# The last 512 queries in two halves, and B's transposing loads held until A's first x has landed

## The chip, the cores and the metric

One core of one Trainium2 chip. The metric is device time in microseconds (us); a kernel is run several times, and the median is quoted with the lowest and highest run. TensorE is PE in the profile, ScalarE is ACT, VectorE is DVE, GpSimd is POOL, SyncE is SP; SPq is the queue on which SyncE issues transfers. L1031 is line 1031 of the kernel's file. The change shifts the lines, so the same statement has another number before and after it: the exponentials are L806 before and L820 after.

## The reference

Two independent attention modules on 2048 positions of 448 columns, set side by side in the output.

```python
def _A_ref(x, wq, wk, wv, wo):        # 16 query heads, one shared key/value head of 28
    q = (x @ wq).reshape(B, S, 16, 28).transpose(0, 2, 1, 3)
    k = x @ wk;  v = x @ wv
    scores = jnp.einsum("bhqd,bkd->bhqk", q, k) * (28 ** -0.5)
    p = _softmax(scores, axis=-1)
    o = jnp.einsum("bhqk,bkd->bhqd", p, v)
    return o.transpose(0, 2, 1, 3).reshape(B, S, 448) @ wo

def _B_ref(x, wqkv, wo):              # window of 8 keys, 2 apart; 16 heads of 28
    ...                               # q, k, v from x @ wqkv; gather; softmax; weighted sum; @ wo

return jnp.concatenate([a, b], axis=-1)
```

A has 16 x 2048 x 2048 exponentials; that is the kernel's main work. B is small and is worked between A's steps.

Some words of the kernel: the scores are the products of queries and keys, PV is the product of the exponentials with the values. A *unit* is one head's scores of 512 queries with 128 keys. A *quad* is four heads with the same 512 queries, 64 units. An *offload* is a tile of exponentials that VectorE works in place of ScalarE. Warm-up matmuls are dummies before the first real one.

## The kernel before

The kernel is a list of operations with their reads `R` and writes `W`; a scheduler with its own model of durations (the second argument of `a(...)`, in us) orders them on each engine and sets the semaphores.

`xst` is A's first 512 rows of x, loaded plainly and transposed by TensorE; the other rows of A's x (`xT_A`) and all of B's (`xT_B`) come by transposing loads of 128x512, four for each chunk of 512 rows, all on SyncE's queue.

```python
        a("act", 0.5, <A_x[0:512] -> xst>, W=["xst"], dsem="i_xa0", ...)
        ...
        a("gp", 1.5, wload(g.wq, g.A_wq, KC, D), ..., dsem="i_wq", ...)       # rest of A's query weights
        for c in range(1, NCH):
            for t in range(4):
                a("sp", 1.05, <transposing load>, R=["xst"], W=[("xT", c, t)], dsem=f"i_xa{c}.{t}", ...)
        for c in range(NCH):
            for t in range(4):
                a("sp", 1.05, <transposing load>, W=[("xT_B", c, t)], dsem=f"i_xb{c}.{t}", ...)
        ...
        a("gp", 1.5, <B's value weights>, W=["wqv"], dsem="i_wbv", land=5, pr=-7, ninc=2)
        ...
        a("sp", 0.6, <zero rows of Vst[0] -> v_dram>, R=[("Vst", 0)], W=[("vd", -1)], dsem="i_vz", land=2.5, pr=3, rel=4)
```

`R=["xst"]` on A's transposing loads is no read: they come from memory. It makes them wait until `xst` has landed, so that they don't take bandwidth from it. `Vst` is a buffer that B's values go through. B's values go through a two-deep buffer `Vst`, whose first slot also serves, zeroed, as the source of the zero rows; and B's products live in the same bytes as `xst`:

```python
        self.xst = self.stage[:, 0:4 * D].rearrange("p (b c) -> p b c", c=D)
        self.prodT = self.stage[:, :].rearrange("p (t w c) -> p t w c", t=4, w=WIN)
        ...
            op = a("dve", t_dve_2x(1024), <product q*k>, R=R, W=[("prodT", t)], pr=pr, rel=T)
            if k == 0:
                op.deps.update(g.s.rd.get("xst", ()))   # the first products overwrite xst
```

The tail of A, before: the last 512 queries of the last four heads are worked like any other quad, 64 units of exponentials and one PV bank (one of the buffers that TensorE's results go to); at the end the normalization is split into two halves of 256 columns, both after the last PV. `OFF_AT` says which exponentials VectorE takes over from ScalarE (66 tiles of 512 columns).

Of the kernel before, what the change touches and what calls it, by code (L numbers as in the profile page):

```python
# [6 lines left out]
ALU = mybir.AluOpType  # L7
# [22 lines left out]
XBANKS = (6, 7)  # L30
TAILB = (0, 1, 2, 4)
WARM = 7
QT = 27.0
# [5 lines left out]
OFF_AT = {q: (0, 2, 5, 7) for q in range(1, 16)}  # L39
OFF_AT.update({q: (0, 2, 3, 5, 7, 8) for q in (5, 9, 13)})  # L40
LATE = 2
# [52 lines left out]
class Sched:  # L94
# [49 lines left out]
    def run(self, engines):  # L144
# [44 lines left out]
        while left:  # L189
# [77 lines left out]
            if e == "pe":  # L267
                if o.use is not None and o.use.spare and o.alone and area(T) < (self.WANT if limit is None or T + o.dur + 0.18 <= limit + self.EPS else self.LOW):
                    o.fill = 1
                    o.dur += 0.18  # L270
                    o.dense += 512 - o.use.spare
                elif (o.full and area(T) < (self.FULL[o.full] if T + 0.22 * o.full + 0.2 <= H + self.EPS else self.LOW)
                      and all(d.start is not None and d.end + self.lat(d) <= T for d in o.opt)):
                    o.deps.update(o.opt)
                    o.dur = 0.22 * o.full
                    o.tiled = False
                    o.dense = 512 * o.full
                elif o.fill is not None:
                    o.full = 0
                    o.fill = max(0, min(0 if waiting else 2, round((self.WANT - area(T)) * self.WIN / 512 + 0.3)))  # L280
                    if T > 14 and area(T) > self.LOW:
                        o.fill = max(0, min(o.fill, int((H - 0.12 - self.MODE - T - o.dur + self.EPS) / 0.22)))
                    o.dur += 0.22 * o.fill
                    o.dense += 512 * o.fill
                if o.tiled and not mode:
                    o.dur += self.MODE
                mode = o.tiled
                if o.dense:
                    recent.append((T + o.dur, o.dense))
                    del recent[:-120]  # L290
# [108 lines left out]
class Gen:  # L399
# [185 lines left out]
    def loads(self):  # L585
# [20 lines left out]
        for c in range(NCH):  # L606
            for t in range(4):
                a("sp", 1.05, one(lambda e, c=c, t=t: e.dma_start(
                    out=g.xT_B[:, t, 512 * c:512 * c + 512], in_=g.B_x[0, 512 * c:512 * c + 512, XB0[t]:XB0[t] + 128],
                    transpose=True)), W=[("xT_B", c, t)], dsem=f"i_xb{c}.{t}", land=4.5, pr=-16 + c)  # L610
        a("sp", 1.2, lambda e: [
# [113 lines left out]
    def a_q(self, sc, first=False):  # L725
# [3 lines left out]
        for t in range(4):  # L729
# [16 lines left out]
            else:  # L746
# [11 lines left out]
              R=["qadd"], W=[("qT", par, t)], use=u, pr=pr if first else -1)  # L758

    def a_loop(self):  # L760
        g, a = self, self.s.add
        units = [(sc, t, tb, j) for sc in range(4) for t in range(4) for tb in range(16) for j in range(4)]
        assert len(units) == NU
        g.last_exp, g.pvs, g.evacs = {}, {}, []
        quads = {(sc, t): [[] for _ in range(4)] for sc in range(4) for t in range(4)}
        dqs = {k: [[] for _ in range(4)] for k in quads}
# [5 lines left out]
        while pos < NU:  # L772
# [9 lines left out]
            def qk(e, us=us, b0=b0, box=[]):  # L782
                for _ in range(box[0].fill):
                    e.matmul(g.bank(b0), g.warm[:, 0:128], g.warm[:, :], start=True, stop=True)
                for i, (sc, t, tb, j) in enumerate(us):
                    if box[0].full:
                        r = e.matmul(g.bank(b0 + i), g.kz[:, j, 128 * tb:128 * tb + 128], g.qT[:, sc % 2, t, :], start=True, stop=True)  # L787
                        continue
                    r = e.matmul(g.bank(b0 + i), g.kT[32 * j:32 * j + 32, 128 * tb:128 * tb + 128],  # L789
                                 g.qT[32 * j:32 * j + 32, sc % 2, t, :], start=True, stop=True, tile_position=(32 * j, 0))  # L790
                return r
            box = []
            o = a("pe", 0.315, lambda e, qk=qk, box=box: qk(e, box=box), R=[("kT", tb // 4) for (_, _, tb, _) in us] + [("qT", sc % 2, t) for (sc, t, _, _) in us],
                  W=[("ring", slot)], pr=-50)
            box.append(o)
            o.ring = o.tiled = True
            o.full = len(us) if len(us) > 1 else 0
            o.opt = {x for (_, _, tb, _) in us for x in g.kz_ops[tb // 4]}
            o.fill = 0
# [10 lines left out]
            for i in range(na):  # L810
                g.last_exp[b0 + i] = x
                quads[us[i][:2]][us[i][3]].append((us[i], ("expT", n % ERING), g.expT[:, n % ERING, 512 * i:512 * i + 512], 0))
            if off:
# [4 lines left out]
            while late and late[0][0] <= n // 2:  # L818
                for x in late.pop(0)[1]:
                    qd = x[0][:2]  # L820
                    g.nq[qd] = g.nq.get(qd, 0) + 1
# [9 lines left out]
            for u in us:  # L831
                js = quads[u[:2]]
                while all(js):
                    g.pv_group([x.pop(0) for x in js])
                if u[2:] == (15, 3):
                    left = [x.pop(0) for x in js if x]
# [3 lines left out]
    def pv_group(self, grp):  # L840
        g, a = self, self.s.add
        qd = grp[0][0][:2]
        all_pv = g.pvs.setdefault(qd, [])
        box = []

        def pv(e):
            for (_, _, tb, j), _, src, w in grp:
                order = [o.seq for o, js in all_pv if j in js]
                first, last = box[0].seq == min(order), box[0].seq == max(order)
                x = e.matmul(g.bank(PVBANK, p0=32 * j, p1=32 * j + 32), g.v_aug[:, w, tb, :], src,  # L850
                             start=first, stop=last, tile_position=(0, 32 * j))
            return x
        o = a("pe", 0.315, pv, R=sorted({y[1] for y in grp}) + sorted(
            {(k, y[3], y[0][2] // 4) for k in ("v_aug", "v_aug1") for y in grp}), pr=-40, dense=700)
        o.tiled = o.pv = True
# [5 lines left out]
        g.npv[qd] = g.npv.get(qd, 0) + len(grp)  # L861
        if g.npv[qd] == 64:
            g.a_quad_end(*qd)

    def offload(self, n, us):

        g = self
        if n % 2 or us[0][:2] != us[-1][:2]:
            return 0
        if us[0][:2] != g.quad:  # L870
            g.quad, g.round = us[0][:2], n // 2
        return int(n // 2 - g.round in OFF_AT.get(4 * us[0][0] + us[0][1], ()))

# [26 lines left out]

    def a_quad_end(self, sc, t):
        g, a = self, self.s.add
        end = 12.0 + QT * (4 * sc + t + 1)
        last = sc == 3 and t == 3
        evacs = []
        hv = 2 if last else 1
        for hf in range(hv):
            w, b = 512 // hv, 16 // hv
            cs, bs = slice(w * hf, w * hf + w), slice(b * hf, b * hf + b)
            keys = [hf] if last else [0, 1]  # L910
            kk = lambda n: [(n, t % 2, x) for x in keys]
            p0 = -30 if last else -1
            o = a("dve", t_dve_ps(w), lambda e, cs=cs: e.transpose(out=g.PV_T[:, t % 2, cs], in_=g.bank(PVBANK)[:, cs]),  # L913
                  W=kk("PV"), pr=-30)
            o.deps.update(x for x, _ in g.pvs[sc, t])
            evacs.append(o)
            pt = g.PV_T[:, t % 2, :].rearrange("p (b e) -> p b e", e=32)
            a("dve", 0.25, lambda e, pt=pt, bs=bs: e.reciprocal(out=g.rden[:, t % 2, bs], in_=pt[:, bs, DH]),
              R=kk("PV"), W=kk("rden"), pr=p0)
            a("dve", t_dve_1x(w), lambda e, pt=pt, bs=bs: e.tensor_tensor(  # L920
                out=g.oN[:, bs, :], in0=pt[:, bs, :], in1=g.rden[:, t % 2, bs].unsqueeze(2).to_broadcast([128, b, 32]), op=ALU.mult),
              R=kk("PV") + kk("rden"), W=[("oN", x) for x in keys], pr=p0)
            a("dve", 0.12 + 1.04e-3 * w, lambda e, cs=cs: e.transpose(
                out=g.oTn[:, t, cs], in_=g.oN[:, :, :].rearrange("p b e -> p (b e)")[:, cs]),
              R=[("oN", x) for x in keys], W=[("oTn", t, x) for x in keys], pr=p0)
        g.evacs = evacs
        pr = end + 20
        if t < 3:
            return
        for s4 in range(4):  # L930
            blk = 4 * sc + s4
            if last:
                u = Use(f"F{sc}.{s4}", (TAILB[s4],), late=True)
            else:
                u = Use(f"F{sc}.{s4}", XBANKS)
            for tt in range(4):
                o = a("pe", t_mm(D), lambda e, u=u, s4=s4, tt=tt: e.matmul(  # L937
                    g.bank(u.bank, D), g.oTn[:, tt, 128 * s4:128 * s4 + 128], g.wo4[:, tt, :], start=tt == 0, stop=tt == 3),
                  R=[("oTn", tt, s4 // 2), "wo4"], W=[u], use=u, pr=pr + s4 + tt if not last else -30 + tt, dense=448)
                if last and tt == 0:  # L940
                    o.deps.add(g.last_exp[TAILB[s4]])
            ob = blk % 4
# [195 lines left out]
```

## Time and profile before

| | before |
|---|---|
| device time, median of the runs | 461.0 us (460.56 to 461.34) |
| profiled span | 459.2 us |
| first exponential starts | 11.29 us |
| last exponential ends | 451.72 us |
| from there to the end | 7.5 us |
| granted TensorE clock | 1.00 |

The prediction below shows how ScalarE is read as the bound. Two more views are needed for what follows. First the timeline of SyncE's queue; the columns are start, length, engine, line, operation, tiles and count:

```profile
5.84 16.61 SPq L603 DMA_TRANSPOSE xT_A<-in_A_x_dram  x12
...
46.46 0.39 SPq L626 DMA_DIRECT2D v_scratch<-Vst  x1
```

Three of B's loads are issued ahead of these twelve (1.9 to 5.8 us), thirteen behind. Each takes 1.30 us of the queue, although the scheduler counts 1.05, and the store of the zero rows comes at 46.46 us.

Second, the DMA view, by queue: packets, MB and share of the 16 engines' time. q1 carries SyncE's transfers, q0 GpSimd's. First 4 to 8 us, then 12 to 14 us:

```profile
q1 hardware_dynamic: 2179, 0.51, 84.2%
```

### The profile page before, as it was taken

To read this page: it belongs to the slowest core of one execution; us is meant where nothing else is said; L and a number is where in the kernel's file an instruction comes from. 1 tells how busy PE (TensorE), PEld (TensorE's weight loads), DVE (VectorE), ACT (ScalarE), POOL (GpSimd) and SP (SyncE) were. 2 spreads that over 40 slices of the span, in tenths; PEclk is the share of its full clock that TensorE was granted. 3 is DMA by queue.
4 is the path that set the end of the run, shared out by engine and by line. 5 is a ranking of instruction groups with operands and counts; after the bars stand their busy time and mean duration, and the time that the engine had idled before them with its cause. 6 is when DMAs were issued, how large, how long until landed. Compare 5 with 4: busy or idle time off the path is not lost.

```text
span 459.2 us, 8717 instructions
## 1 busy us (share of the span) xinstructions
PE 427.7 (93%) x3682; PEld 163.6 (36%) x3682; DVE 380.7 (83%) x622; ACT 444.9 (97%) x430; POOL 9.4 (2%) x29
## 2 busy tenths in 40 slices
PE   8999999999999989999899999899899998989997
PEld 3333232323533324234353342224244342325343
DVE  6556889988798898989688889998988969889883
ACT  3999999999999999999999999999999999999994
POOL 7000000000000000000000000000000000000000
PEclk9999999999999999999999999999999999999999
DMA  7774303002201002020220120002022221214001
GB/s 152 128 162 95 109 27 100 1 1 90 92 15 40 19 10 82 20 81 22 81 91 30 44 83 18 0 13 92 0 97 92 70 78 30 72 31 142 10 1 61
DMA packets 42102, 27.34 MB, mean 60 GB/s; under 512 B 17474, under 2 KB 41904, under 8 KB 42064
## 3 DMA queue, kind: packets, MB, share of 16 engines
q1 hardware_dynamic: 40464, 25.28, 19.6%
q0 software_dynamic: 304, 0.73, 0.6%
q10 hardware_dynamic: 1296, 0.79, 0.5%
q8 instruction: 29, 0.48, 0.4%
q14 instruction: 9, 0.07, 0.1%
HBM read 17.60 MB, written 5.52 MB: 50 GB/s over the span
## 4 chain that ended last, share of the span: by engine, by line
ACT 86%; PE 11%; DVE 1%; DMA 1%; issue 0%
ACT expT L806 85%; PE ps L789 2%; PE ps L1079 2%; PE ps L850 2%; PE ps L787 1%; DMA stage<-in_A_x_dram 1%; PE ps L978 1%; PE ps L1086 1%; PE ps L937 1%; ACT e_t L1054 0%; PE ps L654 0%; PE ps L738 0%; PE ps L1028 0%; PE ps L434 0%; PE ps L993 0%
## 5 line engine op out<-in xcount | busy, mean ns | idle before, releaser
L806 ACT ACTIVATE expT<-ps 128x1024 bf16<-128x1024 f32 (+1 forms) x410 | 438.8, 1209 | 2.1 <-PE ps L789 1.9
L789 PE MATMUL ps<-qT,kT 32*128 32x512 bf16 x824 | 122.3, 385 | 11.6 <-ACT expT L806 9.3
L850 PE MATMUL ps<-expT,v_aug 128*32 128x512 bf16 x958 | 94.8, 389 | 1.0 <-ACT expT L806 1.0
L787 PE MATMUL ps<-qT,kz 128*128 128x512 bf16 x200 | 59.6, 383 | 9.9 <-ACT expT L806 9.4
L789 PEld LDWEIGHTS ps<-qT,kT 32*128 32x128 bf16 x824 | 30.1, 91 | 91.7 <-ACT expT L806 68.4
L883 DVE TENSOR_SCALAR d_x<-ps 128x512 f32<-128x512 f32 x66 | 45.4, 688 | 17.9 <-PE ps L789 16.8
L850 PEld LDWEIGHTS ps<-expT,v_aug 128*32 128x32 bf16 x958 | 24.3, 93 | 62.0 <-issue 55.4
L1073 DVE TENSOR_TENSOR prod<-Vsh,a_n 128x896 bf16<-128x896 bf16 x64 | 37.5, 614 | 7.9 <-PE ps L1079 7.9
L1019 DVE TENSOR_TENSOR stage<-qTB,kTB 112x1024 bf16<-112x1024 bf16 x64 | 42.3, 674 | 1.8 <-PE ps L1028 1.7
L1079 PE MATMUL ps<-ident,prod 128*112 128x128 bf16 x512 | 41.8, 224 | 0.0
L894 DVE SCALAR_TENSOR_TENSOR d_u<-d_u,d_x 128x1024 f32<-128x1024 f32 x33 | 40.1, 1215 | 0.1
L896 DVE SCALAR_TENSOR_TENSOR dexp<-d_u,d_x 128x1024 int16<-128x1024 f32 x33 | 40.0, 1213 | 0.1
L892 DVE SCALAR_TENSOR_TENSOR d_u<-d_x 128x1024 f32<-128x1024 uint16 x33 | 39.9, 1209 | 0.2
L1079 PEld LDWEIGHTS ps<-ident,prod 128*112 128x112 bf16 x512 | 34.2, 130 | 14.7 <-issue 10.9
L978 PE MATMUL ps<-xT_B,wqkv 128*128 128x512 bf16 x128 | 38.9, 383 | 0.0
L787 PEld LDWEIGHTS ps<-qT,kz 128*128 128x128 bf16 x200 | 12.2, 97 | 31.1 <-ACT expT L806 28.9
L1028 PEld LDWEIGHTS ps<-ones,stage 112*128 112x128 bf16 x512 | 18.5, 96 | 7.8 <-issue 4.8
L1028 PE MATMUL ps<-ones,stage 112*128 112x4 bf16 x512 | 21.2, 167 | 0.0
L738 PE MATMUL ps<-xT_A,wq 128*128 128x512 bf16 x64 | 19.8, 384 | 0.1
L1086 PE MATMUL ps<-wo_B,oT 112*128 112x448 bf16 x64 | 18.1, 357 | 0.0
L993 PE MATMUL ps<-wqv,xT_B 128*128 128x448 bf16 x64 | 17.5, 356 | 0.0
L913 DVE STREAM_TRANSPOSE PV_T<-ps 128x512 f32<-128x512 f32 (+1 forms) x17 | 11.4, 676 | 6.7 <-PE ps L850 6.5
(103 smaller groups left out, 303.3 us busy)
## 6 DMA issues: line engine op xcount, KB each, us to landing
Vsh<-v_scratch SPq DMA_DIRECT2D x16, 896.0 KB, 4.6
v_scratch<-Vst SPq DMA_DIRECT2D x16, 112.0 KB, 1.7
out_dram<-outB SPq DMA_DIRECT2D x16, 112.0 KB, 1.7
out_dram<-outA SPq DMA_DIRECT2D x14, 112.0 KB, 1.7
wqkv<-in_B_wqkv_dram SPq DMA_DIRECT2D x1, 672.0 KB, 5.4
stage<-in_A_x_dram ACTq DMA_DIRECT2D x1, 448.0 KB, 4.0
wo_B<-in_B_wo_dram SPq DMA_DIRECT2D x4, 98.0 KB
wo<-in_A_wo_dram SPq DMA_DIRECT2D x4, 98.0 KB
```

The lines of the kernel that those rows point to most:

```text
L787: r = e.matmul(g.bank(b0 + i), g.kz[:, j, 128 * tb:128 * tb + 128], g.qT[:, sc % 2, t, :], start=True, stop=True)
L789: r = e.matmul(g.bank(b0 + i), g.kT[32 * j:32 * j + 32, 128 * tb:128 * tb + 128], g.qT[32 * j:32 * j + 32, sc % 2, t, :], start=True, stop ...
L806: x = a("act", t_exp(w), lambda e, b0=b0, w=w, n=n: e.activation(g.expT[:, n % ERING, 0:w], g.ps[:, 512 * b0:512 * b0 + w], ACT.Exp, scale ...
L850: x = e.matmul(g.bank(PVBANK, p0=32 * j, p1=32 * j + 32), g.v_aug[:, w, tb, :], src, start=first, stop=last, tile_position=(0, 32 * j))
L883: o = a("dve", t_dve_ps(512), lambda e: e.tensor_scalar(out=xx[:, 512 * h:512 * h + 512], in0=g.bank(bank), scalar1=-128.0 * A2, scalar2=1 ...
L892: a("dve", t_dve_1x(1024), lambda e: e.scalar_tensor_tensor(out=u, in0=lo, scalar=EP * F, in1=lo, op0=ALU.add, op1=ALU.mult), R=di, W=["d_ ...
L894: a("dve", t_dve_1x(1024), lambda e: e.scalar_tensor_tensor(out=v, in0=u, scalar=EQ * F * F, in1=lo, op0=ALU.add, op1=ALU.mult), R=["d_u"] ...
L896: a("dve", t_dve_1x(1024), lambda e: e.scalar_tensor_tensor(out=out, in0=v, scalar=EL / F ** 3, in1=xx, op0=ALU.mult, op1=ALU.subtract), R ...
L978: a("pe", t_mm(512), lambda e, u=u, t=t, kt=kt, w=w: e.matmul(g.bank(u.bank), g.wqkv[:, kt, w * D + KC * t:w * D + KC * t + 128], g.xT_B[: ...
L1019: op = a("dve", t_dve_2x(1024), lambda e, t=t, qv=qv, kv=kv: e.tensor_tensor(out=g.prodT[0:KC, t, :, :], in0=qv, in1=kv, op=ALU.mult), R=R ...
L1028: r = e.matmul(g.bank(u.bank, 128).rearrange("p (h w) -> p h w", w=WIN)[:, 4 * t:4 * t + 4, w], g.prodT[0:KC, t, w, :], g.ones4[:, :], sta ...
L1079: a("pe", 0.056, lambda e, u=u, t=t, w=w: e.matmul(g.bank(u.bank, 128, 128 * t, p1=KC), g.prod2[:, w, KC * t:KC * t + KC], g.ident[:, :], ...
```

## The change

Its intent is to shorten both ends of the kernel. At the end, the last 512 queries of the last four heads become two halves of 256 queries, so that PV, normalization and output of the first half run beside the scores of the second, and only 256 columns are left after the last exponential. At the start, B's transposing loads get the same hold as A's. With it come fewer offloads (62), two more warm-up matmuls and a rule of the scheduler's model.

```diff
-TAILB = (0, 1, 2, 4)
-WARM = 7
+TAILB = (4, 0)
+WARM = 9
...
-OFF_AT.update({q: (0, 2, 3, 5, 7, 8) for q in (5, 9, 13)})
+OFF_AT.update({q: (0, 2, 3, 5, 7, 8) for q in (7,)})
+OFF_AT[15] = (0, 2, 3, 5)
...
-                if o.tiled and not mode:
+                if o.tiled and (not mode or o.fill):
                     o.dur += self.MODE
...
-                    transpose=True)), W=[("xT_B", c, t)], dsem=f"i_xb{c}.{t}", land=4.5, pr=-16 + c)
+                    transpose=True)), R=["xst"], W=[("xT_B", c, t)], dsem=f"i_xb{c}.{t}", land=4.5, pr=-16 + c)
...
+    def key(self, u):
+        return (3, 3, u[2] // 8) if u[:2] == (3, 3) else u[:2]
+    def parts(self, u):
+        if u[:2] == (3, 3):
+            return [(2 * (u[2] % 8) + i, 256 * (u[2] // 8), 256) for i in range(2)]
+        return [(u[2], 0, 512)]
... (scores, PV and the end of a quad go over parts(u) and key(u); the end of a quad takes hf = None, 0 or 1)
```

## The prediction

> **What bounds the kernel now.** I began with the page of the kernel before: busy time per engine, the row of ACT in the 40 slices, the chain that ended last, and the costliest group.
>
> ```profile
> PE 427.7 (93%) x3682; PEld 163.6 (36%) x3682; DVE 380.7 (83%) x622; ACT 444.9 (97%) x430; POOL 9.4 (2%) x29
> ...
> ACT  3999999999999999999999999999999999999994
> ...
> ACT 86%; PE 11%; DVE 1%; DMA 1%; issue 0%
> ...
> L806 ACT ACTIVATE expT<-ps 128x1024 bf16<-128x1024 f32 (+1 forms) x410 | 438.8, 1209 | 2.1 <-PE ps L789 1.9
> ```
>
> ScalarE (ACT) runs 410 exponentials and is idle 2.1 us around them, 1.9 of which come before the first. So the time has three parts: a **head** up to the first exponential, a **stream** of exponentials, and a **tail** after the last one. The timeline, cut to ACT, gives the borders, and the timeline of the last 8 us gives the tail:
>
> ```profile
> 11.29 5.97 ACT L806 ACTIVATE expT<-ps 128x1536 bf16<-128x1536 f32 x5 [1.90 <-PE ps L789]
> ...
> 434.81 16.91 ACT L806 ACTIVATE expT<-ps 128x1024 bf16<-128x1024 f32 x16
> ```
>
> ```profile
> 451.95 0.40 PE L850 MATMUL ps<-expT,v_aug 128*32 128x512 bf16 x4
> ...
> 452.41 0.78 DVE L913 STREAM_TRANSPOSE PV_T<-ps 128x256 f32<-128x256 f32 x2 [5.22 <-PE ps L850]
> 453.11 0.32 DVE L918 RECIPROCAL rden<-PV_T 128x8 f32<-128x8 f32 x2
> 453.34 0.72 DVE L920 TENSOR_TENSOR oN<-PV_T,rden 128x256 bf16<-128x256 f32 x2
> 453.99 0.76 DVE L923 STREAM_TRANSPOSE oTn<-oN 128x256 bf16<-128x256 bf16 x2
> 454.48 0.11 PEld L937 LDWEIGHTS ps<-wo,oTn 128*128 128x128 bf16 x2 [0.46 <-DVE oTn L923]
> ...
> 454.67 0.65 DVE L1082 CAST oT<-ps 112x512 bf16<-112x512 f32 x1
> ...
> 455.25 1.14 DVE L947 CAST outA<-ps 128x448 bf16<-128x448 f32 x2
> ...
> 456.35 0.62 DVE L1089 CAST outB<-ps 128x448 bf16<-128x448 f32 x1
> 457.00 0.33 SPq L1091 DMA_DIRECT2D out_dram<-outB  x1
> ```
>
> Head 11.29 us; stream 11.29 to 451.72 = 440.43 us; tail 451.72 to 459.2 = 7.5 us. In the tail VectorE (DVE) is the path: it works two 256-column halves of the last PV bank one beside the other, then the last evacuations of module B (oT, outB) queue with those of outA, and the outB store is the last thing issued.
>
> A second look at the stream matters, since a busy ACT can hide a wait. Within runs of exponentials the start-to-start times in the trace are 904 ns (1024 columns) and 1330 ns (1536) at their medians. 270 x 0.904 + 139 x 1.330 = 429.0 us; the stream ends another 0.7 us after the last start, so about 10.7 us of the 440.4 are not plain exponentials. Eight e_t exponentials (0.30 each) and four gcol ones explain about 3. The other 6 us sit in some 70 places of 0.03 to 0.25 us where the score matmuls ended later than 120 ns before the exponential could have begun. ACT waits for PE a little, and counts it as busy.
>
> **What the Trainium skill says.** "ScalarE: Activation LUTs", What ACT_TABLE_LOAD costs: an ACTIVATE streams one element per 0.833 ns, with a fixed part that back-to-back ones partly hide. The trace agrees: 1330 - 904 = 426 ns for 512 more columns, 0.832 each, so 50 ns per exponential is fixed. "TensorE: Matmul & The Clock Gate", Back-to-back issue gap: a warm matmul costs N/2.4 + 2.5 ns when it follows another, so halving one into two 256-column ones is nearly free (an estimate from that page: 218 against 216 ns); the trace has no 256-column matmul, but two full-array 512-column score matmuls start 215 to 225 ns apart. "TensorEngine Tiling (Array Packing)", Key Properties: tiles work independently; in the trace three 32-row score matmuls start within 7 ns and all end 0.39 us after the first start. "DMA: Bandwidth & Descriptors", Issuing engines are not separate DMA queues: all queues share the 16 engines; the trace agrees, below.
>
> **The change, part by part.**
>
> *Head.* Three transposing loads of B's x no longer run before A's first x has landed. The DMA view of the kernel before, cut to 3.4 to 3.9 us and then to 4.4 to 4.9 us (packets, MB, share of 16 engines; q10 carries the load of x, q1 the transposes):
>
> ```profile
> q10 hardware_dynamic: 225, 0.19, 108.7%
> q1 hardware_dynamic: 9, 0.00, 1.1%
> ```
>
> ```profile
> q1 hardware_dynamic: 256, 0.06, 64.2%
> q10 hardware_dynamic: 315, 0.07, 61.3%
> ```
>
> As the transposes arrive, q10 falls from 0.19 to 0.07 MB per half microsecond. Between 3.9 and 4.82 us it moved 0.16 + 0.07 MB; at 0.19 per half that is 0.6 us instead of 0.92, so x should land 0.3 us sooner. The 16 PE transposes, which wait for it 0.5 us, follow. The order of the built program also puts the four Q projections ahead of the second K projection, with two warm-up matmuls in the gap; worth about 0.1. A's later transposing loads start a microsecond sooner, which nothing waits for. Head: **-0.4 us**. B's loads come later, but their first use is at 38.0 us, and in the new order it still stands before the 25th exponential.
>
> *Stream.* Offloaded exponentials on DVE fall from 66 to 62: two fewer in each of quads 5, 9 and 13, two more in 7 (the last quad keeps four, all in its first half). Counted in the built program: 143 exponentials of 1536 and 266 of 1024 against 139 and 270. Four go from 904 to 1330 ns: 4 x 0.426 = **+1.7 us**. DVE loses 4 x 0.69 + 2 x (1.21 + 1.215 + 1.213) = 10 us, but beside ACT, so that is worth only what it takes off PE's waits.
>
> *Waits inside the stream.* In the last 32 units of two key blocks, a tiled score group is six 256-column matmuls, the two halves of one head one after the other in the same 32 rows. If they stagger in order I estimate 0.39 + 2 x 0.107 = 0.60 us. From the end of the exponential that frees the banks, a prompt group needs 0.055 + 0.60 + 0.046 = 0.70 us, and has 904 - 111 = 0.79 (the 111 is how far an exponential's record runs past the start of the next). It fits by 0.09, where a 512-column one has 0.30. But the median tiled group in the trace starts 0.23 us after the banks are free, because PE is finishing something else: such a one would now cost ACT about 0.1. Some 13 tiled groups, with PE freer than before (B's last work now stands before them): **+0.4 us**. Against it, less DVE work and a scheduler that counts a mode switch after each filler should take something off the 6 us: **-0.3 us**, the softest number here.
>
> *Tail.* Only 256 columns remain. From the end of the last exponential E: PV starts at +0.23 and DVE at +0.69 as before (eight 256-column PV matmuls in two rounds of four end when four of 512 do). Then one half alone: 0.41 + 0.16 + 0.39 + 0.43 with three 0.04 us gaps = 1.5, so oTn is ready at E+2.2 (before: E+2.7 and E+3.0). Last output matmuls +0.4; copies on ACT and DVE beside each other 0.6; the last store is issued at about E+3.4. Before it was 457.00 - 451.72 = E+5.3. From issue to the end stays 2.2 us. Tail: 5.6 instead of 7.5, **-1.9 us**. Module B's last 10 transposing matmuls, oT, projection and outB are gone from here: the order shows them before the second half.
>
> Sum: -0.4 + 1.7 + 0.4 - 0.3 - 1.9 = -0.5, from 461.0 to **460.5 us**.
>
> **The rivals.** (1) *The longer score groups stall ACT at every second exponential.* For it: 0.09 us of slack, and the schedule still takes them for 0.315 us long. Against it: with B gone PE idles before most groups, so they start promptly. Cost: up to 13 x 0.25 = 3 us, giving 463. (2) *The whole program is reordered, and the 6 us of small waits change.* Each is a near miss between two engines, so a new order draws new ones; the sign is open, the size perhaps 1 us each way, giving 459.5 to 461.5. (3) *The tail is hidden by another end*: if B's last store or the first half's outputs still came after E+3.4, the saving would vanish and the time be 462. The order speaks against it: B's last projection stands 21 score groups before the end. (4) *DVE sets the boundary between the halves*: the first half's last PV needs two DVE exponential chains (3.7 us each), and PE is in order, so a late chain blocks scores. I counted about 1 us to spare (chain done near 4.8 us after its scores, wanted at 5.7). Cost if late: about 1 us.
>
> **Range and chances.** The two large terms, +1.7 and -1.9, are counted and nearly cancel. The head is good to 0.3, the tail to 0.4, the small waits to about 1: 459.3 to 461.9 us eight times in ten. A 2% change is 9.2 us, as much as the whole tail and more; nothing in the change can give or take it. Within 2%: 0.98; 0.01 on each side.
>
> **What would show it.** First exponential at 10.9 us, and x landed near 4.5. 410 exponentials, the spacing sum up by 1.7. From the end of the last exponential to the end of the span 5.6 us, with outA as the last store and no L1098 or L1101 in the tail. Six-matmul score groups about 0.60 us long, and no idle time of ACT at the border of the halves. I am wrong if those groups cost ACT over 1 us in sum, if the small waits elsewhere move by more than 1.5 us, or if the head does not move.

## More of the kernel before

What an operation has to wait for comes from this rule:

```python
    def add(self, eng, dur, emit, R=(), W=(), pr=0.0, rel=0.0, ..., dsem=None, land=0.0, ...):
        for k in R:
            if k in self.wr:
                op.deps.add(self.wr[k])            # a reader waits for the last writer
            self.rd.setdefault(k, []).append(op)   # ... and is entered as a reader
        for k in W:
            ...
            op.deps.update(self.rd.get(k, ()))     # a writer waits for all readers
```

The loads that matter here.

```profile
q1 hardware_dynamic: 1181, 0.28, 73.6%
q0 software_dynamic: 83, 0.20, 31.6%
```

Between 4 and 8 us the transposes, most of them B's three, keep the DMA engines busy. This looks like interference with A's x, and is what the change wants to remove.

## The result, and the profile after

| | before | after |
|---|---|---|
| median of the runs | 461.0 us (460.56 to 461.34, 6 runs) | 465.57 us (464.8 to 469.8, 6 runs) |
| profiled span | 459.2 us | 462.8 us |
| first exponential starts | 11.29 us | 11.37 us |
| last exponential ends | 451.72 us | 457.08 us |
| from there to the end | 7.5 us | 5.8 us |
| granted TensorE clock, all runs | 1.00 | 0.976 to 0.999 |

The ratio is 1.0113, 95% interval 1.0076 to 1.015. Here and below a ratio is the mean time of one kernel's fast runs over that of the other's of the same rounds, so it is not quite the ratio of the medians. The changed kernel is slower by 1.1%, inside 2%, but outside the predicted range. Its times also spread over 5 us, where the kernel before spreads over 0.8.

The tail is as predicted. The timelines of ScalarE's last exponentials, and of VectorE behind them:

```profile
439.50 17.57 ACT L820 ACTIVATE expT<-ps 128x1024 bf16<-128x1024 f32 x16
```

```profile
457.58 0.45 DVE L926 STREAM_TRANSPOSE PV_T<-ps 128x256 f32<-128x256 f32 x1 [5.45 <-PE ps L866]
...
458.77 0.45 DVE L935 STREAM_TRANSPOSE oTn<-oN 128x256 bf16<-128x256 bf16 x1
...
459.67 0.62 DVE L959 CAST outA<-ps 128x448 bf16<-128x448 f32 x1 [0.46 <-PE ps L949]
```

One chain of 256 columns, then outA; nothing of module B is left there. The loss must lie in the stream (the exponentials between the first and the last). The costliest group of the page has grown an idle part (after the bar: idle time before the group, and what ended most of it):

```profile
L820 ACT ACTIVATE expT<-ps 128x1024 bf16<-128x1024 f32 (+1 forms) x410 | 440.2, 1231 | 6.0 <-PE ps L803 5.7
```

It was 2.1, of which 1.9 came before the first exponential. ScalarE's timeline from 44 us says where the rest is; the number in brackets is idle time just before:

```profile
50.10 2.52 ACT L820 ACTIVATE expT<-ps 128x1536 bf16<-128x1536 f32 x2 [2.68 <-PE ps L803]
53.94 6.46 ACT L820 ACTIVATE expT<-ps 128x1536 bf16<-128x1536 f32 x6 [1.31 <-PE ps L803]
```

Both waits name PE. PE's and VectorE's waits, and VectorE's timeline, lead further back:

```profile
PE ps L795 <- DVE d_x L899: 2.9, 1, 2.9
```

```profile
46.19 0.69 DVE L1031 TENSOR_TENSOR stage<-qTB,kTB 112x1024 bf16<-112x1024 bf16 x1 [2.89 <-DMA xT_B<-in_B_x_dram]
...
48.10 0.68 DVE L899 TENSOR_SCALAR d_x<-ps 128x512 f32<-128x512 f32 x1
```

Read upwards: ScalarE waits for scores, PE (which works in order) waits for VectorE to read a score bank at L899, and VectorE (in order too) sits 2.89 us in front of L1031, B's first product, until the *last* of B's transposing loads has landed. The product has no use for that load: its own operands were copied before. It waits because the hold entered B's sixteen loads as readers of `xst`, and the first product, which overwrites `xst`, waits for all readers. In the kernel before, VectorE came to the same product 7 us later, behind its first copy of B's values, and neither waited:

```profile
51.89 0.61 DVE L997 CAST Vst<-ps 128x448 bf16<-128x448 f32 x1
...
53.08 0.68 DVE L1019 TENSOR_TENSOR stage<-qTB,kTB 112x1024 bf16<-112x1024 bf16 x1
```

The second gap, 1.31 us, follows from the first. In the windows view (stretch; then busy us and count of PE, PEld, DVE, ACT, POOL; then PE's granted clock, DMA share, GB/s):

```profile
46.00:50.00 4.00, 1.10 (x10) 0.23 (x8) 3.81 (x7) 1.42 (x2) 0.00 (x0) 0.73 0.54 136
50.00:54.00 4.00, 4.00 (x20) 0.82 (x17) 2.24 (x3) 2.54 (x3) 0.00 (x0) 0.50 0.25 70
```

In the first stretch PE was busy 1.10 of 4 us and its clock fell to half; in the second it was busy all the time and still too slow. The trace's record of the granted clock has the fall at 47.85 us and full clock again at 54.68. "TensorE: Matmul & The Clock Gate", What's actually happening, has this state: half clock after an idle window of about 3.4 us, full clock after as long a busy one. The trace agrees with the half clock (0.50) and with the length: the 6.83 us at half clock are two times 3.41, and PE was busy 2.34 us of the first and all of the second.

SyncE's queue shows the same delay of everything behind the loads:

```profile
49.45 0.39 SPq L627 DMA_DIRECT2D v_scratch<-Vst  x1
```

That is 3.0 us later than before. This line plays a part only later.

To see losses in one number per stretch I took, from each trace, the start-to-start times of neighbouring exponentials and summed what goes beyond 904 ns (after one of 1024 columns) or 1330 ns (after one of 1536), by the stretch in which the later one starts. This "excess" is used for all experiments:

| excess, us | to 24 us | 24 to 45 | 45 to 60 | 60 to 80 | after 80 | sum |
|---|---|---|---|---|---|---|
| before | 0.1 | 0.6 | 0.3 | 0.3 | 9.4 | 10.7 |
| after | 0.1 | 0.9 | 4.4 | 0.5 | 8.5 | 14.5 |

After 80 us the changed kernel has even a little less. Nearly all that it lost is between 45 and 60 us.

### The profile page after: what moved, and what is told of

Read it like the earlier page. It is cut to its first block, busy times and chain, and to the rows that moved or that the text cites. A ratio compares the mean times of both kernels' runs of the same rounds, so it can differ in the third digit from the quotient of the medians.

```text
span 462.8 us, 8908 instructions
## 1 busy us (share of the span) xinstructions
PE 422.6 (91%) x3747; PEld 165.7 (36%) x3802; DVE 372.6 (81%) x613; ACT 445.8 (96%) x429; POOL 9.4 (2%) x29
## 4 chain that ended last, share of the span: by engine, by line
ACT 80%; PE 9%; SPq 8%; DMA 2%; DVE 1%; issue 0%; DVEq 0%
ACT expT L820 79%; SPq L609 4%; SPq L604 3%; PE ps L803 2%; PE ps L866 2%; PE ps L1091 1%; PE ps L800 1%; DMA stage<-in_A_x_dram 1%; PE ps L990 1%; DMA xT_B<-in_B_x_dram 1%; PE ps L1040 1%; ACT e_t L1066 1%; PE ps L1005 0%; PE ps L949 0%; PE ps L1098 0%
## 5 line engine op out<-in xcount | busy, mean ns | idle before, releaser
L803 PE MATMUL ps<-qT,kT 32*128 32x512 bf16 (+1 forms) x853 | 120.3, 375 | 13.0 <-ACT expT L820 10.8
L866 PE MATMUL ps<-expT,v_aug 128*32 128x512 bf16 (+1 forms) x1022 | 95.8, 378 | 0.7 <-DVE v_aug L718 0.5
L800 PE MATMUL ps<-qT,kz 128*128 128x512 bf16 (+1 forms) x204 | 57.6, 362 | 13.4 <-ACT expT L820 10.2
L899 DVE TENSOR_SCALAR d_x<-ps 128x512 f32<-128x512 f32 x62 | 42.7, 688 | 24.4 <-PE ps L803 23.5
L1031 DVE TENSOR_TENSOR stage<-qTB,kTB 112x1024 bf16<-112x1024 bf16 x64 | 42.6, 677 | 3.6 <-DMA xT_B<-in_B_x_dram 2.9
L1091 PE MATMUL ps<-ident,prod 128*112 128x128 bf16 x512 | 44.7, 225 | 0.0
L910 DVE SCALAR_TENSOR_TENSOR d_u<-d_u,d_x 128x1024 f32<-128x1024 f32 x31 | 37.7, 1215 | 0.2
L908 DVE SCALAR_TENSOR_TENSOR d_u<-d_x 128x1024 f32<-128x1024 uint16 x31 | 37.7, 1215 | 0.1
L912 DVE SCALAR_TENSOR_TENSOR dexp<-d_u,d_x 128x1024 int16<-128x1024 f32 x31 | 37.6, 1214 | 0.1
L990 PE MATMUL ps<-xT_B,wqkv 128*128 128x512 bf16 x118 | 36.8, 383 | 0.7 <-issue 0.6
L800 PEld LDWEIGHTS ps<-qT,kz 128*128 128x128 bf16 x235 | 15.3, 97 | 30.1 <-ACT expT L820 26.3
```

What stands on the lines that cost most here:

```text
L800: r = e.matmul(g.bank(b0 + i, nq, nq * k), g.kz[:, j, 128 * tb:128 * tb + 128], g.qT[:, sc % 2, t, q0:q0 + nq], start=True, stop=True)
L803: r = e.matmul(g.bank(b0 + i, nq, nq * k), g.kT[32 * j:32 * j + 32, 128 * tb:128 * tb + 128], g.qT[32 * j:32 * j + 32, sc % 2, t, q0:q0 + ...
L866: x = e.matmul(g.bank(PVBANK, nq, q0, p0=32 * j, p1=32 * j + 32), g.v_aug[:, w, tb, :], src[:, nq * k:nq * k + nq], start=first, stop=last ...
L899: o = a("dve", t_dve_ps(512), lambda e: e.tensor_scalar(out=xx[:, 512 * h:512 * h + 512], in0=g.bank(bank), scalar1=-128.0 * A2, scalar2=1 ...
L908: a("dve", t_dve_1x(1024), lambda e: e.scalar_tensor_tensor(out=u, in0=lo, scalar=EP * F, in1=lo, op0=ALU.add, op1=ALU.mult), R=di, W=["d_ ...
L910: a("dve", t_dve_1x(1024), lambda e: e.scalar_tensor_tensor(out=v, in0=u, scalar=EQ * F * F, in1=lo, op0=ALU.add, op1=ALU.mult), R=["d_u"] ...
```

## The experiments

All kernels gave correct results. Medians and ranges are of all runs; ratios leave out runs over 1.5% above the fastest of their kernel, which are the slowest run of e10 and that of e11. The kernel before was timed on the same chip in the same rounds; its median there was 460.69 to 460.9 us. In e1, e2, e3, e5, e10, e11 and e13 to e15 every engine but SyncE keeps the order of instructions of the kernel that is edited; the others are scheduled anew.

### Is it the first product's wait? (e1_narrow, e2_wait15)

The theory: the wait at L1031 is the whole loss. e1 lets the product wait only for TensorE's reads of `xst`, which are the real ones; e2 leaves out only the very last load.

```diff
-                op.deps.update(g.s.rd.get("xst", ()))
+                op.deps.update(o for o in g.s.rd.get("xst", ()) if o.eng == "pe")      # e1_narrow
+                op.deps.update(o for o in ... if o.dsem != "i_xb3.3")                  # e2_wait15
```

> The changed kernel with one wait taken away: the first product of module B (prodT, into the buffer that x was staged in) waits only for the sixteen PE transposes that really read that buffer, and no longer for the sixteen transposing loads that were entered as readers of it only to hold them back. The instruction order of every engine is the same as in the changed kernel. Theory (false wait): VectorE no longer idles 2.9 us near 43 us, ACT has no gap of 2.7 and 1.3 us near 48 and 53 us, TensorE keeps its full clock: about 461.0 us (465.6 less 4.0 to 4.5). Rival (the loads themselves come too late, or share the DMA engines with something that is needed): stays at 464.5 or more, since the loads are issued at the same times. Rival (halves, other order): stays at 464.5 or more.

> The changed kernel with the last of the sixteen transposing loads left out of the wait of the first product; same order on every engine. Theory (false wait): the 15th load lands about 1.3 us before the 16th, so VectorE idles about 1.5 us instead of 2.9; ACT had about 1 us of slack there, so it loses 0.3 to 1 us and TensorE idles too briefly to fall to half clock: 461.3 to 462.0 us. If the loss were proportional to the wait: 463. If the wait doesn't matter: 465.

Measured: e1 464.79 us (463.27 to 466.55), ratio 1.0098; e2 464.3 us (463.55 to 466.08), ratio 1.0081. VectorE's wait for the load is gone from both profiles, and the time hardly moved. The excess moved instead: e1 has 2.5 us before 24 us and 1.6 us between 45 and 60 (behind a wait of VectorE that e11 explains below), e2 has 4.8 us before 24 us. So the theory was only part of the story: a gap that opened elsewhere took the place of the one removed.

### The hold without the rest (e3_before_hold, e4_before_hold_warm9)

The kernel before plus the one line of the hold; e4 adds the two warm-up matmuls, which give the scheduler another order (B's first product is then the 65th instruction of VectorE in the trace instead of the 78th).

```diff
-                    transpose=True)), W=[("xT_B", c, t)], ...
+                    transpose=True)), R=["xst"], W=[("xT_B", c, t)], ...
-WARM = 7
+WARM = 9        # e4 alone
```

> The kernel before with the hold alone (all transposing loads of B's x wait for A's first x). The order on PE, ACT, VectorE is that of the kernel before; only the DMA queue's order changes. The first product now waits for all sixteen loads too, but in this order it stands 14 VectorE instructions later, near 53 us, and the loads have landed by 47 us. Theory (false wait that matters only with the new order): no stall, 460.8 to 461.1 us, with the first exponential at about 11.2 us. Rival (the hold by itself costs 4 us): 465.

> The kernel before with the hold and with nine warm-up matmuls instead of seven, nothing else. In the built order the two warm-ups make the scheduler put the first product of module B 14 VectorE instructions earlier, as in the changed kernel. Theory (hold and order together): the same stall of VectorE near 43 us and of ACT near 48 us, 464 to 466 us. Rival (the split of the last queries or the offloads cost the 4 us): 461.

Measured: e3 462.05 us (461.39 to 464.16), ratio 1.0034, interval 1.0009 to 1.006; e4 465.58 us (465.32 to 465.75), ratio 1.0102. e4's number is the expected one, but the expected stall is not what made it. Its trace has 3.9 us of excess before 24 us, a wait at the first product of 0.9 us in place of 2.9, and a tail of 9.6 us in place of 7.5, because in the order built for it B's last output comes behind A's. So e4 can't serve as proof of the first product's wait. e3 is cleaner: the hold alone costs time even in the old order, where the first product comes too late to wait. e3's trace (its slowest run, 464.16) has 4.1 us of excess before 24 us. ScalarE's timeline and PE's waits there:

```profile
17.71 1.45 ACT L806 ACTIVATE expT<-ps 128x1536 bf16<-128x1536 f32 x1 [2.44 <-PE ps L789]
```

```profile
PE ps L667 <- DMA xT_A<-in_A_x_dram: 2.6, 2, 1.5
```

A's *own* transposing loads arrive late, though they are issued 0.8 us sooner than before. The DMA view of e3, 4 to 8 us and then 12 to 14 us, answers to that of the kernel before:

```profile
q1 hardware_dynamic: 706, 0.16, 21.6%
```

```profile
q0 software_dynamic: 64, 0.21, 78.4%
q1 hardware_dynamic: 224, 0.05, 29.4%
```

Before, B's three loads moved while the DMA engines had little else to do: 0.51 MB by transposes in 4 to 8 us, against 0.16 now. Once they are held, A's loads are the first transposes. Both before and after, A's loads meet GpSimd's two weight loads (A's remaining query weights and B's value weights) in 9 to 16 us; in e3 they come off worse. In 12 to 14 us GpSimd's queue moves as much as before, 0.2 MB, but takes 78% of the engines' time for it instead of 32%, and the transposes move 0.05 MB instead of 0.28. By the landing events in the trace, the third and fourth load of A's first chunk land at 14.9 and 16.8 us, against 13.4 and 14.1 before. Issued sooner, landed later.

### Take the contention away (e5_hold_wqv_later), and the order alone (e6_warm9_alone)

e5 is e3 with B's value weights, not needed before 45 us, held until A's first chunk has landed. e6 has 9 warm-ups without the hold: e4's order of VectorE up to its 226th instruction, past B's first product, and another one behind that.

```diff
-          W=["wqv"], dsem="i_wbv", land=5, pr=-7, ninc=2)
+          R=[("xT", 1, 3)], W=["wqv"], dsem="i_wbv", land=5, pr=-7, ninc=2)        # e5
```

> The kernel before with the hold, and GpSimd's load of B's value weights held until the first chunk of A's transposed x has landed; every engine keeps its order. Contention theory: in the run with the hold alone the transposing loads moved 0.15 to 0.17 MB before 8 us where the kernel before moved 0.52 MB, so they met GpSimd's two weight loads in 9 to 16 us, and the chunk's third and fourth load landed at 14.9 and 16.8 us against 13.4 and 14.1 us. With the value weights out of the way they land at or before 14 us, ScalarE has no gap of over 1 us before 20 us, and the time is 460.0 to 461.0 us, at or under the kernel before. Rival (late landings come from something else, or the loss of the hold is not in the head): about 462.0 us as before.

> The kernel before with 9 warm-up matmuls in place of 7 and so the changed kernel's order of instructions on each engine; no hold, no halves, 66 offloads. If the new order itself costs (it asks for A's chunks some matmul groups sooner), 461.5 to 463 us, with ScalarE gaps of over 0.5 us before 22 us. If the order only hurts together with the hold, 460.7 us, within 0.3 us of the kernel before.

Measured: e5 460.98 us (460.49 to 462.62), ratio 1.0007; the two loads landed at 13.8 and 14.1 us, and the excess before 24 us is 0.15 us. e6 460.67 us (460.3 to 460.84), ratio 0.9997. So the late loads need the value weights' load beside them, and they are most likely what the hold costs in the old order; the profiles, one of each, differ clearly, while the intervals of the two ratios overlap a little. The new order of the head alone costs nothing.

### The halves and the offloads by themselves (e7_halves_alone, e8_offload62_alone)

e7 has the halves, but no hold, 7 warm-ups, the old rule of the model and the 66 offloads of before; e8 is the kernel before with 62 offloads:

```diff
-OFF_AT.update({q: (0, 2, 3, 5, 7, 8) for q in (5, 9, 13)})
+OFF_AT.update({q: (0, 2, 3, 5, 7, 8) for q in (7,)})           # e8
```

> The last 512 queries in halves and nothing else of the change: no hold, 7 warm-ups, 66 offloads, the old rule for the tile mode. The profile of the changed kernel has the tail 1.8 us shorter (5.7 against 7.5 us), so 458.7 to 459.3 us if the halves bring what the tail shows. Rival: the smaller matmul groups of the halves cost the stream as much as the tail gains: 460.5 to 461 us.

> The kernel before with 62 offloaded tiles of exponentials in place of 66: four more tiles of 512 columns on ScalarE, worth 1.7 us by the prediction (four times 427 ns). If ScalarE is the bound as the prediction has it, 462.1 to 462.7 us. If VectorE or TensorE takes part in the bound, the freed VectorE work gives some of it back: 460.7 to 461.7 us.

Measured: e7 461.75 us (461.72 to 461.76), ratio 1.002: a miss, I expected a gain of 1.8. Its stream is as long as before (last exponential's end at 451.27 us), but its tail is 8.5 us. VectorE's timeline in it:

```profile
453.02 0.62 DVE L1101 CAST outB<-ps 128x448 bf16<-128x448 f32 x1
...
455.30 0.68 DVE L1094 CAST oT<-ps 112x512 bf16<-112x512 f32 x1
...
457.00 0.62 DVE L1101 CAST outB<-ps 128x448 bf16<-128x448 f32 x1 [0.45 <-PE ps L1098]
```

With 66 offloads VectorE comes to B's last two outputs only behind the last exponential, where PE works 32 small matmuls and two projections for them between those of A. The halves don't bring their gain unless B is out of the way. e8: 461.45 us (460.96 to 462.56), ratio 1.0016, so 0.75 us instead of the 1.7 that the added exponentials take by themselves. Its trace says where the difference is: the stream is 1.1 us longer, since the excess falls by 0.4, and the tail is 7.0 us, since B's last output is no longer in it. So the four offloads that were given up are the price for the short tail, and part of that price comes back.

### The change without the hold, and the two repairs on it (e9, e10, e11, e12)

```diff
# e9_no_hold: the changed kernel, with the hold taken back
-                    transpose=True)), R=["xst"], W=[("xT_B", c, t)], ...
+                    transpose=True)), W=[("xT_B", c, t)], ...
# e10_wqv_later: the changed kernel, value weights held as in e5
# e11_narrow_and_wqv_later: e1's edit and e5's edit
# e12_no_hold_64: e9 with  OFF_AT.update({q: (0, 2, 3, 5, 7, 8) for q in (5, 9)})
```

> The changed kernel less the hold alone: halves, 62 offloads, 9 warm-ups and the rule for the tile mode stay. Theory (the hold is the whole of the loss): the four offloads measured 0.75 us, the tail is then 7.1 us and becomes 5.7 us, so 460.7 + 0.75 - 1.4 = 460.1 us, 459.6 to 460.6. Rival (the halves themselves stretch the stream, as the 461.75 us of the halves alone could also mean): 461.5 us or more.

> The changed kernel with GpSimd's load of B's value weights held until the first chunk of A's transposed x has landed, every engine's order unchanged. Only the contention is taken away; VectorE's wait for the 16 transposing loads near 46 us stays with its 2.7 plus 1.3 us of idle ScalarE, less what slack there is. Two separate causes: 462.5 to 464 us, ScalarE gaps near 48 and 53 us only. If the contention is all: 460 to 461 us. If it plays no part here: 465 us and gaps before 22 us.

> Both repairs at once, order unchanged: VectorE's first product waits only for TensorE's reads of the buffer, and the value weights load is held until A's first chunk has landed. Two causes: 459.6 to 460.6 us, at the level of the changed kernel without the hold, with no ScalarE gap of over 1 us between the first and the last exponential. If something else of the change costs the time, 462 us or more.

> A version meant to beat both: the changed kernel without the hold and with 64 offloads (six each in the third quarter's two quads numbered 5 and 9, none beyond that late in the stream). Two offloads more are worth 0.4 to 0.85 us against the same kernel with 62, if VectorE's work for B still ends before the last exponential: 459.3 to 459.9 us. If B's last products come after the last exponential again, as in the halves alone with 66, 461 us or more.

Measured: e9 460.43 us (460.05 to 460.75), ratio 0.999, interval 0.9977 to 1.0003: everything but the hold costs nothing, the hold is the whole loss, 1.2% or 5.7 us by the two ratios. (e9 was scheduled anew, and VectorE's order differs from its 357th instruction on; e13 below confirms it in the changed kernel's own order.) e10 464.41 us (462.59 to 466.42, and a slow run of 470.38), ratio 1.0071. e11 466.19 us (461.99 to 467.32, and a slow run of 470.91), ratio 1.01: a clear miss. Neither has a gap before 24 us any more, and e11 has no wait at L1031. But e11's trace has a gap of 2.45 us before 54.47 us, and this is behind it, in PE's and VectorE's waits:

```profile
PE ps L990 <- DVE Vst L1009: 3.2, 1, 3.2
```

```profile
DVE Vst L1009 <- DMA v_scratch<-Vst: 3.2, 1, 3.2
```

A third wait of the same parent. VectorE's first copy of B's values goes into slot 0 of `Vst`, from which the store of the zero rows reads; the store stands on SyncE's queue behind all loads, and the hold has pushed it from 46.5 to 49.6 us. In the kernel before the copy came at 51.9 us, so nothing was seen; in the changed kernel as it is, the stall at L1031 kept the copy back for long enough. Only with that stall repaired or shorter did this wait show: 3.2 us in e11, 2.1 in e1, 0.6 in e2. These three have the same order on VectorE, and their excess before 24 us runs the other way: 0.1, 2.5 and 4.8 us. The later the stream already runs, the shorter this wait. e12: 460.76 us (460.46 to 461.27), ratio 0.9999, no gain: its tail is 7.0 us, with an outB of B in it again. Its profile also has 1.3 us of the wait for the zero rows' store, without any hold; moving that store was not tried without the hold.

### All three repaired, and one left in at a time (e13, e14, e15)

The third repair moves the zero rows' store ahead of B's loads on SyncE's queue.

```diff
-          R=[("Vst", 0)], W=[("vd", -1)], dsem="i_vz", land=2.5, pr=3, rel=4)
+          R=[("Vst", 0)], W=[("vd", -1)], dsem="i_vz", land=2.5, pr=-16.8, rel=4)
```

e13 has this and the edits of e1 and e5; e14 leaves out e5's edit, e15 leaves out e1's. Together with e11, which leaves out this one, each wait has one run in which it alone is left.

> The changed kernel with the hold and three repairs: the first product waits for TensorE's reads alone, the value weights load waits for A's first chunk, and the zero rows' store is issued ahead of B's transposing loads in place of behind them; the order on all engines but SyncE's queue is unchanged. If the three waits are all of the loss: 459.8 to 460.8 us, like the changed kernel without the hold, and excess of the exponentials' spacing below 2 us in all before 80 us. If there is a fourth cause in the hold: 462 us or more.

> As the run with three repairs, but the value weights load is free again, so that only the late first-chunk loads of A are left. Three causes: 2.5 to 4.8 us of excess spacing between 14 and 24 us as in the earlier runs with it, so 462.5 to 465 us where it falls out so, and no gap of over 1 us after 24 us. Rival (contention matters only by pushing the later stages into the other two waits): 461 us or less.

> As the run with three repairs, but the first product waits for all sixteen of B's transposing loads again. Three causes: VectorE waits 2.9 us or more for the last load (0.4 us later now, the store ahead of it), ScalarE loses 4 to 5 us between 45 and 60 us as in the run with the value weights later alone: 463.5 to 465 us. Rival (that stall was only there because of the zero rows' store): 461 us or less.

| kernel | median (lowest to highest), us | ratio | 95% interval |
|---|---|---|---|
| e13, all three repaired | 460.48 (459.4 to 461.56) | 0.999 | 0.9974 to 1.0006 |
| e14, contention left | 462.67 (459.9 to 464.13) | 1.0028 | 1.0003 to 1.0054 |
| e15, first product left | 465.2 (462.47 to 465.95) | 1.0088 | 1.0071 to 1.0104 |
| e11, zero rows' store left | 466.19 (461.99 to 467.32, slow 470.91) | 1.01 | 1.007 to 1.013 |
| the changed kernel | 465.57 (464.8 to 469.8) | 1.0113 | 1.0076 to 1.015 |

With all three repaired the hold is free: the time is that of e9, and in e13's trace ScalarE idles nowhere between the first and the last exponential by more than its usual small waits. The store now stands ahead of the sixteen loads, and VectorE's copy is out at 48.8 us; SyncE's and VectorE's timelines:

```profile
20.68 0.61 SPq L627 DMA_DIRECT2D v_scratch<-Vst  x1
```

```profile
48.79 0.62 DVE L1009 CAST Vst<-ps 128x448 bf16<-128x448 f32 x1 [0.28 <-PE ps L1005]
```

By the difference of the ratios to 0.999, times 460.8 us, the contention alone costs 1.8 us, the first product alone 4.5 us, the zero rows' store alone 5.1 us. The first is the least certain, since the intervals of e13 and e14 overlap a little. They don't add up to the 5.7 us of the hold: an early stall gives the transfers time to catch up, so that a later one shrinks, as e11, e1 and e2 show. The excess of one profiled run each, which is not always a typical one:

| excess, us | to 24 us | 24 to 45 | 45 to 60 | 60 to 80 | after 80 |
|---|---|---|---|---|---|
| e3, hold alone, old order | 4.1 | 0.6 | 0.3 | 0.3 | 9.4 |
| e5, the same with value weights later | 0.2 | 0.6 | 0.3 | 0.3 | 9.4 |
| e9, change without the hold | 0.5 | 1.4 | 0.1 | 0.7 | 8.0 |
| e13, three repairs | 0.2 | 0.9 | 0.1 | 0.7 | 8.4 |
| e14, contention left | 1.0 | 0.9 | 0.1 | 0.7 | 8.4 |
| e15, first product left | 0.2 | 0.9 | 2.3 | 0.5 | 8.5 |
| e11, zero rows' store left | 0.1 | 0.9 | 3.6 | 2.0 | 8.8 |

e14's and e15's profiles were of their faster runs (460.47 and 462.47 us), so they show less than the medians say. What differs is TensorE's clock. The profiles of the changed kernel, e2, e10 and e11 have 6.83 us at half clock behind the stall, those of e1, e3 and e4 3.41 us, those of e14 and e15 none. In e11 it is from 54.68 to 61.51 us, which is where its loss between 60 and 80 us is from. VectorE waits about as long at the first product in e15 (2.7 us) as in the changed kernel (2.9 us), but between 45 and 60 us the excess is 2.3 us at full clock and 4.4 with the half clock. The timed runs fit: e14's two runs at a granted clock of 1.00 took 459.9 and 460.47 us, its four at 0.992 to 0.995 took 462.17 to 464.13. So much of what a stall costs, and of the spread from run to run, goes with whether PE loses its clock behind it. No run varied the clock by itself, so this is read from the traces and not tested.

### A version without the hold that keeps 64 offloads (e16_64_B_earlier)

e12 with B's steps planned 22.8 us apart instead of 23.6, which brings B's last output ahead of the second half's chain.

```diff
-    BSTEP = 23.6
+    BSTEP = 22.8
```

> The changed kernel without the hold, with 64 offloads and B's steps planned 22.8 instead of 23.6 us apart, which puts B's last output copy ahead of the second half's chain on VectorE. If the tail is then 5.8 us as without the hold and the two offloads save their 0.4 to 0.85 us: 459.5 to 460.1 us, 0.9985 or less of the kernel before. If B's earlier steps meet other work and stretch the stream: 460.5 us or more.

Measured: 460.34 us (460.02 to 460.79), ratio 0.9988, interval 0.9975 to 1.0. The tail is 6.0 us. It is the lowest median of all, by 0.35 us against the kernel before in the same rounds (460.69); the interval touches 1, so a gain is likely but not shown. What the halves can win is nearly used up by the offloads they need.

## Why the prediction was wrong, by its own steps

- **The step that failed** stands in its head: "A's later transposing loads start a microsecond sooner, which nothing waits for", and "B's loads come later, but their first use is at 38.0 us, and in the new order it still stands before the 25th exponential". The hold was weighed as a matter of the head alone, and for the rest only by asking when PE first *reads* the loaded data. Three other things hang on these loads. They share the DMA engines, so A's loads, issued sooner, could land later, and TensorE waited for them (e3 against e5: 4.1 against 0.2 us of excess before 24 us). They are entered as readers of a buffer that a later operation overwrites, so VectorE waited for the last of them (2.7 us in e15, which lost 4.5). And they share an in-order queue, so a small store behind them came 3 us later (e11, which lost 5.1). PE does use B's data in time; I checked those reads alone, and the losses lay elsewhere.
- **The head, -0.4: its first step is not there.** x landed at 4.71 instead of 4.83 us in the two profiles; in all of them it landed between 4.70 and 5.07 us with the hold and between 4.70 and 5.05 without. The load of x ran at 0.04 to 0.15 MB per half microsecond at its end even without B's transposes, so most of the fall that I put down to them was the load running out. The first exponential came at 11.37 us. In the other profiles it came between 10.35 and 12.44 us with the hold and between 10.63 and 11.58 without. It goes with the moment at which TensorE got its full clock: 6.89 us in the changed kernel and 7.07 in the one before (first exponential at 11.37 and 11.29), 4.79 in e1 (10.43), 9.15 in e5 (12.44). PE's sixteen transposes took 1.89 us in the changed kernel's profile and 1.07 in e1's, which has the same order. The prediction had no such term, and a gain of a tenth or two can't be read beside it.
- **The stream, +1.7: right in kind, too large in effect.** The counts are as predicted, 143 and 266 and one short one. Measured alone (e8) the four offloads cost 0.75 us, since freed VectorE time shortened other waits (-0.4) and the tail (-0.4). I had -0.3 for the first, and counted the second under the halves.
- **The score groups, +0.4: wrong, and harmless.** I estimated 0.60 us for six 256-column matmuls. They take 0.40, as three of 512 do, and the excess in the last 30 us of the stream is 0.6 us against 0.8 before. Rival 1 fell with this. PE's timeline in the changed kernel:

```profile
428.95 0.40 PE L803 MATMUL ps<-qT,kT 32*128 32x256 bf16 x6
```

- **The tail, -1.9: right.** 5.8 us against a predicted 5.6. But e7 shows that the reason given is only half of it: without fewer offloads B's work stays in the tail, and the halves gain nothing. The order of the built program showed B in front, and I took that for an effect of the halves.
- **Rivals 2 to 4.** The small waits of the stream did not grow (excess after 80 us 8.5 against 9.4). B's last store did not come after A's. No gap of ScalarE stands at the border of the halves.
- Without the hold the sum was close: 460.5 less the head's -0.4 is 460.9, and e9 measured 460.43. This is partly luck: the offloads came out 0.3 us (1.1 in the stream against +1.7 - 0.3) and the score groups 0.4 us better than summed, the tail 0.2 worse, and e9's first exponential fell early (10.63 us).

Three things stay open. Why GpSimd's transfers take two and a half times as much of the DMA engines' time for the same bytes in e3 is not known. Nor is how often this hit the timed runs. Of the six profiles with the hold and the value weights at their old place, the fourth load of A's first chunk landed at 16.3 to 16.8 us in three (e2, e3, e4), and at 13.8 to 14.7 in the changed kernel, e1 and e14, no later than in the profiles without the hold (14.1 to 14.9). e1 and e14 still have 2.5 and 1.0 us of excess before 24 us; their first exponential came early, at 10.4 and 10.5 us, so that they needed the loads sooner. With the value weights moved the load landed at 12.6 to 14.1 us, and no profile has more than 0.2 us of this excess. And the rule of the scheduler's model was never tested alone.

## What to carry to other kernels

When a transfer is held back, ask of three things what it delays: its consumers, everything behind it on its queue, and every operation that must wait for it as a *user of a buffer*. An ordering edge entered as a false read can cost nothing where it is added and stop another engine much later; better to give it a name of its own. B's three early transfers cost nothing in their stretch (e9, without the hold, lost nothing), and moving them put others in the way of something that was not waiting before. A stall can cost more than its length, where TensorE loses its clock behind it. And where a repair moves the time little, look where the gap went before giving up the cause: here three waits covered each other, and only the run with all of them repaired, with one left in at a time, settled it.

## What the Trainium skill lacked or had wrong

- "DMA: Bandwidth & Descriptors", Latency and other measured facts, gives a transposing load's bandwidth (261 GB/s). What issuing one takes of the queue stands only in the page's trn3 part, as cycles for small tiles on "previous generations", not for this size. Here one load of 512x128 two-byte elements keeps SyncE's queue for 1.26 to 1.30 us, 131 KB in that time or some 100 GB/s, so sixteen of them hold it for 21 us.
- The same page, Issuing engines are not separate DMA queues, is right that the queues share the 16 engines, but has no figure for what two queues do to each other: GpSimd's 0.2 MB took 32% of the engines' time between 12 and 14 us in the kernel before and 78% in e3, while the transposes fell from 0.28 to 0.05 MB.
- "TensorE: Matmul & The Clock Gate", What's actually happening, speaks of an idle window. Here PE was not idle all through: in the 3.41 us before the clock fell it was busy 1.59 us in the changed kernel, 0.96 in e11 and 1.94 in e3, and it then stayed at half clock for 6.83, 6.83 and 3.41 us. What share of busy time is enough to keep the clock is not said.
- No page says how two column halves behave in the same rows of a tiled group: six 32-row matmuls of 256 columns took 0.40 us, no longer than three of 512.
